# Decode attention in two parts: other half buffers for the sliding-block part, and the last keys loaded ahead of the last three value chunks

## Chip, cores, metric

One core of one Trainium2 chip. The metric is the device time of one execution in microseconds (us); the profiled span is 1.7 to 2 us shorter than the time of the same run. All runs quoted were in the fast state; the granted clock (the share of PE's full clock that the chip let it have, mean of a run) was 0.93 to 0.94.

The names in the profile: PE is the matrix engine, which does products and transposes; DVE and ACT copy and do the other arithmetic; SP issues the loads, and 16 transfer engines carry each of them. In brackets after an instruction stands the idle time before it and what ended it; "issue" means that the engine waited for nothing that the profile shows.

## The reference, cut to what matters

```python
# part A: 4 batches, 32 query heads on 8 key/value heads, the last 2048 of 8192 positions
k = jnp.repeat(k_cache[:, :, Sk - W:, :], rep, axis=1)
v = jnp.repeat(v_cache[:, :, Sk - W:, :], rep, axis=1)
scores = jnp.einsum("bhqd,bhkd->bhqk", q, k) * (Dh ** -0.5)
p = _softmax(scores, axis=-1)
o = jnp.einsum("bhqk,bhkd->bhqd", p, v)        # then @ wo
# part B: the same with 32 key/value heads and all 8192 positions
return jnp.concatenate([a, b], axis=-1)
```

One query position a batch, so every key and value is read once: 570 MB in bf16, and 587 MB with the weights. The time is that of a stream, if the stream never stops: 1366 us at the 430 GB/s of before's full slices.

## The kernel before: the parts that matter

The work is cut into 72 chunks: 0 to 7 are part A (2 MB of keys, 2 MB of values each), 8 to 71 are part B (4 MB and 4 MB). One tensor `kv` of ten half buffers (2 MB each) holds all loads in flight. An A load takes one half, from a list; a B load takes two, keys in 0-1 or 2-3, values in 4-5 or 6-7, by turns. Halves 8 and 9 serve only A and the first query weights.

```python
HALF_A = {"k": (3, 8, 0, 1, 2), "v": (7, 9, 4, 5, 6)}

def take(load, at, n, release):          # a load waits for what last read its halves
    waits = []
    for i in range(at, at + n):
        waits += held[i]
        held[i] = [release]
    half_of[load] = at
    return waits

def dma_kv(kind, c):
    ...
    at = HALF_A[kind][c % 5] if ch["ab"] == 0 else (0 if kind == "k" else 4) + 2 * (c % 2)
    waits = take((kind, c), at, 1 if ch["ab"] == 0 else 2,
                 ("T", ch["s_last"]) if kind == "k" else ("pv", c))
    ...      # the values of chunk 71 come in four pieces: LASTV = (64, 32, 16, 16) of 128 tiles

loads = [("k", c + 1) for c in range(NC - 1)]
for c in range(NC):
    loads.insert(2 * c + 1, ("v", c))     # k1 v0 k2 v1 ... k71 v70 v71
```

SP issues all these loads in this order. Keys are released by `("T", ...)`, the last transpose of the chunk on PE; values by `("pv", c)`, the last product with them. For each chunk PE does `keys_part(c)` (128 transposes in B, 64 in A, 8 to a group, each group copied out by DVE or ACT, and the scores two groups behind), then `values_part(c - 1, c)` (the products of the chunk before, with the last scores and the softmax statistics of this one in between):

```python
for c in range(NC):
    keys_part(c)
    ...
    values_part(c - 1 if c else None, c)
emit_wos(NC - 1)
norm_sum(NC - 1)
for g in range(chunks[NC - 1]["NG"]):
    emit_pv(NC - 1, g)
pv_done(NC - 1)
emit_fin(NC - 1)
```

PE's program is a loop over the periods of two chunks that are alike (`sch.mark()` at every even B chunk); what comes before chunk 12 and from chunk 70 on stands as straight code.

Of the kernel before, what the change touches and what calls it, by code (L numbers as in the profile page):

```python
# [116 lines left out]
def bass_concat_heads__sliding_block_cached__mha_block_cached__decode_kernel(  # L117
# [23 lines left out]
    chunks = []  # L141
# [6 lines left out]
    NC = len(chunks)  # L148
    NCA = Hkv
# [21 lines left out]
    with ExitStack() as es:  # L171
# [65 lines left out]

        half_of = {}
        held = [[] for _ in range(NH)]
        HALF_A = {"k": (3, 8, 0, 1, 2), "v": (7, 9, 4, 5, 6)}  # L240

        def take(load, at, n, release):
            waits = []
# [53 lines left out]

        loads = [("k", c + 1) for c in range(NC - 1)]
        for c in range(NC):
            loads.insert(2 * c + 1, ("v", c))  # L300
        wo_next = 0
        for kind, c in loads:
            dma_kv(kind, c)
# [22 lines left out]
        def emit_xT():  # L326
            for ab in (0, 1):
                xv = xs[:, ab, :].rearrange("b (p r) -> b r p", r=KC)
                for r in range(KC):
                    o = xtps[:, (ab * KC + r) * NB:(ab * KC + r + 1) * NB]  # L330
                    pe_mm(o, xv[:, r, :], identb[0:NB, 0:NB], transpose=True,
                          waits=[("x", 0), ("x", 1), "c_identb"], key="xTmm" if (ab == 1 and r == KC - 1) else None)
            sch.add("dve", lambda e: e.tensor_copy(xT[:, :, :], xtps.rearrange("p (a x) -> p a x", a=2)),
                    waits=["xTmm"], key="xT")
            ms_read[:] = ["xT"]
# [59 lines left out]
        def emit_S(s):  # L395
            c, g = groups[s]
            ch = chunks[c]
            for t in range(TG):
                j = g * TG + t
                if ch["ab"] == 1:  # L400
                    bank, o0 = c % 2, 2 * j
                else:
                    bank, o0 = j // HT, 16 * (j % HT)

                n = min(NW, 512 - o0)
                q = qb[:, c % 2, 0:n] if ch["ab"] == 1 else qs[:, 16 * ch["g"]:16 * ch["g"] + n]
                waits = []
                if t == 0:
                    waits = [("ev", s)] + sc_read[bank]
                    if g == 0:  # L410
                        waits += [("qb", c) if ch["ab"] == 1 else ("q", 0)]
                    sc_read[bank] = []
                pe_mm(sc[:, bank, o0:o0 + n], kt[:, s % NKT, t * P:(t + 1) * P], q,
                      waits=waits, key=("S", s) if t == TG - 1 else None)
# [22 lines left out]
        def stats_rowmax(c):  # L437
            ch = chunks[c]
            m, C = c % NSM, ch["C"]
            if ch["ab"] == 0:  # L440
                src = sA[:, c % 2, :].rearrange("p (j c) -> p c j", c=C)
                sch.add("dve", lambda e: e.tensor_reduce(out=rm[:, m, 0:C], in_=src, axis=AX.X, op=ALU.max),  # L442
                        waits=[("so", c, 0), ("so", c, 1)], key=("rowmax", c))
                return
            for u, pp in HALVES:
                src = sc[pp, c % 2, 0:NTB * 2].rearrange("p (j u) -> p u j", u=2)[:, u, :]
                sch.add("dve", lambda e, src=src, pp=pp: e.tensor_reduce(out=rm[pp, m, 0:1], in_=src, axis=AX.X, op=ALU.max),  # L447
                        waits=[("S", ch["s_last"])], key=("rowmax", c) if u == 1 else None)
# [58 lines left out]
        def emit_pv(c, g):  # L507
            ch = chunks[c]
            UC = ch["UC"]
            base = 16 * (c % NSM) if ch["ab"] == 0 else 2 * ((c - NCA) % 2)  # L510
            for t in range(TG):
                j = g * TG + t
                n = NW if c < NC - 1 else UC
                waits = [("exp", c)] + po_read if j == 0 else []
                if c == NC - 1:
                    waits += [("vl", j)] if ("vl", j) in sch.tk else []
                elif j == 0:
                    waits += [("v", c)]
                pe_mm(po[:, base:base + n], tile_of("v", c, j), pbt[ch["ab"]][:, c % NPB, j * UC:j * UC + n],
                      start=j == 0, stop=j == ch["NT"] - 1, waits=waits, key=("pv", c) if j == ch["NT"] - 1 else None)  # L520
# [31 lines left out]
        def emit_fin(c):  # L552
            ch = chunks[c]
            ab = ch["ab"]
            p0 = 0 if ab == 1 else 32
            if ab == 1:
                ov = oz[:, :].rearrange("p (b u) -> p b u", u=2)
                ops = [(ov[:, :, u], wos[:, u, :]) for u in range(2)]
                waits = [("oT", c), ("wos", c)]
            else:  # L560
                w = wor[:, ch["wo"] % NWO, :].rearrange("p (hl n) -> p hl n", hl=4)
                ov = oT[:, c % NSM, :].rearrange("p (u c) -> p u c", c=REP)
                ops = [(ov[:, :, cc], w[:, cc, :]) for cc in range(REP)]
                waits = [("oT", c), ("wo", ch["wo"])]
            lastc = NC - 1 if ab == 1 else NCA - 1
            firstc = NCA + 1 if ab == 1 else 0
            for i, (l, r) in enumerate(ops):
                pe_mm(fin[p0:p0 + NB, :], l, r, start=i == 0 and c == firstc, stop=i == len(ops) - 1 and c == lastc,
                      waits=waits if i == 0 else [], key=("fin", c) if i == len(ops) - 1 else None)
            if c == lastc:  # L570
                sch.add("dve", lambda e: e.tensor_copy(outsb[p0:p0 + NB, :], fin[p0:p0 + NB, :]), waits=[("fin", c)], key=("osb", ab))
                sch.add_dma("sp" if ab == 1 else "act",
                            lambda e: e.dma_start(out[:, 0, ab * DO:(ab + 1) * DO], outsb[p0:p0 + NB, :]),
                            "d_o%d" % ab, waits=[("osb", ab)], key=("out", ab))


        def pv_done(c):
            if c < NCA or (c - NCA) % 2:
                norm_out(c)

        def keys_part(c):
            ch = chunks[c]
            if c >= NCA and (c - NCA) % 2 == 0:
                sch.mark()
            for g in range(ch["NG"]):
                emit_T(ch["s"] + g)
                if g >= SLAG:
                    emit_S(ch["s"] + g - SLAG)
                if ch["ab"] == 0 and g == HT // TG - 1 + SLAG:
                    scores_out(c, 0)  # L590

                if 1 <= c <= NCA and g == 2:
                    stats_gmax(c - 1)
                if 1 <= c <= NCA and g == 3:
                    stats_exp(c - 1)
                if 1 <= c <= NCA and g == 6:
                    norm_sum(c - 1)
                if 2 <= c <= NCA + 1 and g == 4:
                    emit_fin(c - 2)
                if c > NCA + 1 and (c - NCA) % 2 == 0 and g == 4:  # L600
                    emit_wos(c - 1)
                if c > NCA + 1 and (c - NCA) % 2 == 0 and g == 6:
                    norm_sum(c - 1)
                if c > NCA + 2 and (c - NCA) % 2 == 1 and g == 4:
                    emit_fin(c - 2)

        def values_part(c, nxt):

            ch = chunks[nxt]
            late = list(range(ch["s_last"] + 1 - SLAG, ch["s_last"] + 1))  # L610
            todo = {2: lambda: emit_S(late[0]), 5: lambda: scores_last(nxt)}
            if ch["ab"] == 1:
                todo[10] = lambda: stats_gmax(nxt)
                todo[14] = lambda: stats_exp(nxt)
            if nxt + 1 < NC and nxt + 1 >= NCA:
                todo[7] = lambda: emit_qb(nxt + 1)

            def scores_last(c):
                emit_S(late[1])
                if chunks[c]["ab"] == 0:  # L620
                    scores_out(c, 1)
                stats_rowmax(c)

            for g in range(16):
                if c is not None and g < chunks[c]["NG"]:
                    emit_pv(c, g)
                    if g == chunks[c]["NG"] - 1:
                        pv_done(c)
                if g in todo:
                    todo[g]()  # L630

        emit_xT()
        emit_q(0)
        for c in range(NC):
            keys_part(c)
            if c == 0:
                emit_q(1)
            values_part(c - 1 if c else None, c)
        emit_wos(NC - 1)
        norm_sum(NC - 1)  # L640
        for g in range(chunks[NC - 1]["NG"]):
            emit_pv(NC - 1, g)
        pv_done(NC - 1)
        emit_fin(NC - 1)

        @block.sync
# [54 lines left out]
```

## Time and profile before

| | before |
|---|---|
| time, median of 4 runs beside the change | 1403.47 us (1402.05 to 1403.87) |
| profiled span (of another run, 1404.69 us) | 1402.8 us |
| busy: PE, DVE, ACT | 84%, 48%, 30% |
| HBM read, mean rate over the span | 587.21 MB, 419 GB/s |
| keys 8 landed / values 8 landed | 130.5 / 162.3 us |
| values 70 landed / last piece of values 71 landed | 1385.6 / 1395.4 us |
| last product with values 71 done | 1399.0 us |

"Landed" is the last of the 16 increments that a load leaves in the trace, one for each transfer engine (in before 16 packets of SP's loads were in flight for 88% of the time); the engines are not level, and the slowest sets it (values 70 in before: first increment at 1376.7 us, last at 1385.6). The profile's lines are in the prediction below. PE's speed changes too: in before its granted clock was 0.50 from 1376 to 1380 us, where the first 24 transposes of chunk 71 took 2.74 us, and 1.00 from 1356.5 to 1358, where 24 of chunk 70 took 1.51. Read the row of GB/s first: where it stands at 430 (425 to 435 in slices 6 to 39) the stream sets the time, the transfer engines' busy share being 1.00 to 1.01 from 160 to 1380 us, and a gain must come from the slices where it does not.

### The profile page before, as it was taken

The numbers are of one execution on the slowest core, as the hardware profiler recorded it, in microseconds if no ns is written. First come the engines' busy times: TensorE is split into PE (matmuls) and PEld (weight loads), VectorE is DVE, ScalarE is ACT, GpSimd is POOL, SyncE is SP. The second block draws the span as 40 slices with busy tenths as digits, with TensorE's granted clock in tenths as the row PEclk, the third lists the DMA queues.
The fourth block names the chain that finished last, engine by engine and source line by source line (L and its number), as shares of the span: only waits on it lengthen the run. The fifth ranks groups of instructions, "written<-read, shape, count | busy, mean of one in ns | idle before, by whom it ended". The sixth has DMA issues, their size and how long they took to land.

```text
span 1402.8 us, 57072 instructions
## 1 busy us (share of the span) xinstructions
PE 1175.2 (84%) x26768; PEld 1133.0 (81%) x26768; DVE 673.4 (48%) x1327; ACT 423.3 (30%) x617; POOL 19.2 (1%) x22
## 2 busy tenths in 40 slices
PE   4876796989888898888888888888988798888887
PEld 4765786888888898888888888888988788888887
DVE  2775453544444454444544444444544354444553
ACT  1332232333323233223332233323333233223331
POOL 1111000000000000000000000000000000000000
PEclk9998998999999999999999999999999999999998
DMA  9997899999999999999999999999999999999995
GB/s 400 416 413 286 357 429 428 432 432 425 431 430 433 430 433 430 431 428 434 432 431 430 428 432 433 434 427 430 432 431 433 429 430 433 433 426 435 431 431 251
DMA packets 29992, 588.02 MB, mean 419 GB/s; under 512 B 2656, under 2 KB 10864, under 8 KB 11120
## 3 DMA queue, kind: packets, MB, share of 16 engines
q1 hardware_dynamic: 29912, 587.22, 98.0%
q8 instruction: 40, 0.66, 0.2%
q14 instruction: 16, 0.13, 0.0%
q10 hardware_dynamic: 24, 0.01, 0.0%
HBM read 587.21 MB, written 0.01 MB: 419 GB/s over the span
## 4 chain that ended last, share of the span: by engine, by line
DMA 62%; PE 33%; DVE 4%; issue 1%; ACT 0%; SPq 0%; ACTq 0%; DVEq 0%
DMA kv<-in_B_k_cache_dram 59%; PE tr L320 20%; PE sc L322 9%; PE po L322 2%; DMA kv<-in_A_k_cache_dram 1%; PE fin L322 1%; DMA kv<-in_A_wq_dram 1%; DVE kt L383 1%; DVE rsa L500 1%; DVE sA L432 1%; PE ms L322 1%; DVE sel L425 1%; DVE rm L442 0%; DVE sA L489 0%; DVE rs L498 0%
## 5 line engine op out<-in xcount | busy, mean ns | idle before, releaser
L320 PE MATMUL tr<-identb,kv 128*128 128x128 bf16 x8704 | 705.1, 232 | 176.6 <-DMA kv<-in_B_k_cache_dram 168.5
L383 DVE COPY kt<-tr 128x1024 bf16<-128x1024 bf16 x736 | 502.8, 691 | 491.8 <-PE tr L320 487.5
L320 PEld LDWEIGHTS tr<-identb,kv 128*128 128x128 bf16 x8704 | 560.2, 105 | 203.2 <-issue 110.9
L381 ACT ACTIVATE kt<-tr 128x1024 bf16<-128x1024 bf16 x352 | 360.5, 1024 | 668.7 <-PE tr L320 666.1
L322 PE MATMUL sc<-qb,kt 128*128 128x64 bf16 x8192 | 424.7, 197 | 0.9 <-DVE kt L383 0.7
L322 PEld LDWEIGHTS sc<-qb,kt 128*128 128x128 bf16 x8192 | 351.4, 101 | 2.8 <-DVE kt L383 0.9
L322 PE MATMUL po<-pbb,kv 128*128 128x64 bf16 (+1 forms) x8192 | 290.1, 191 | 12.5 <-issue 12.3
L322 PEld LDWEIGHTS po<-pbb,kv 128*128 128x128 bf16 x8192 | 263.0, 97 | 13.2 <-issue 11.1
L481 ACT ACTIVATE pbb<-sc,negb 64x128 bf16<-64x128 f32 x128 | 51.2, 400 | 297.8 <-DVE negb L471 297.0
L447 DVE TENSOR_REDUCE rm<-sc 64x1 f32<-64x128 f32 x128 | 37.0, 289 | 94.1 <-PE sc L322 93.2
L322 PE MATMUL sc<-qs,kt 128*128 128x64 bf16 (+3 forms) x512 | 26.3, 197 | 16.5 <-DVE kt L383 16.5
L471 DVE COPY negb<-ms 128x1 f32<-128x1 f32 (+1 forms) x72 | 11.4, 159 | 56.6 <-PE ms L322 56.6
L322 PEld LDWEIGHTS sc<-qs,kt 128*128 128x128 bf16 x512 | 21.2, 101 | 19.6 <-DVE kt L383 19.4
L459 DVE TENSOR_REDUCE gm<-ms 1x2 f32<-1x128 f32 (+1 forms) x72 | 20.1, 278 | 31.9 <-PE ms L320 31.7
L322 PE MATMUL ms<-identf,gx 1*128 1x1 f32 (+1 forms) x144 | 27.6, 259 | 0.8 <-DVE gx L463 0.8
L322 PEld LDWEIGHTS ms<-identf,gx 1*128 1x128 f32 (+1 forms) x144 | 21.5, 186 | 5.1 <-DVE gx L463 1.1
L481 ACT ACTIVATION_READ_ACCUMULATOR pbb<-sc,negb 64x1 f32 x128 | 23.7, 185 | 0.0
L322 PE MATMUL po<-pba,kv 128*128 128x64 bf16 x512 | 20.0, 197 | 0.0
L322 PE MATMUL fin<-wos,oz 128*4 128x512 bf16 x64 | 19.6, 388 | 0.3 <-DVE oz L541 0.3
L320 PE MATMUL ms<-identf,rm 128*1 128x128 f32 (+1 forms) x72 | 19.6, 273 | 0.2 <-DVE rm L447 0.2
L322 PEld LDWEIGHTS po<-pba,kv 128*128 128x128 bf16 x512 | 17.6, 101 | 0.0
L432 DVE TENSOR_REDUCE sA<-sel 128x128 f32<-128x512 f32 x16 | 17.0, 1061 | 0.5
(46 smaller groups left out, 179.4 us busy)
## 6 DMA issues: line engine op xcount, KB each, us to landing
kv<-in_B_k_cache_dram SPq DMA_DIRECT2D x64, 4096.0 KB, 27.5
kv<-in_B_v_cache_dram SPq DMA_DIRECT2D x63, 4096.0 KB, 32.1
kv<-in_A_k_cache_dram SPq DMA_DIRECT2D x8, 2048.0 KB, 25.8
kv<-in_A_v_cache_dram SPq DMA_DIRECT2D x8, 2048.0 KB, 25.5
kv<-in_A_wq_dram SPq DMA_DIRECT2D x1, 4096.0 KB, 12.3
kv<-in_B_wq_dram SPq DMA_DIRECT2D x1, 4096.0 KB, 27.2
wor<-in_A_wo_dram SPq DMA_DIRECT2D x8, 512.0 KB, 21.3
wor<-in_B_wo_dram SPq DMA_DIRECT2D x8, 512.0 KB, 33.3
```

The costliest lines, as they stand in the source:

```text
L320: emit = lambda e: e.transpose(o, l, r)
L322: emit = lambda e: e.matmul(o, l, r, start=start, stop=stop)
L381: sch.add("act", lambda e: e.activation(dst, src, ACTF.Copy), waits=waits, key=("ev", s))
L383: sch.add("dve", lambda e: e.tensor_copy(dst, src), waits=waits, key=("ev", s))
L425: sch.add("dve", lambda e: e.tensor_tensor(out=sel[:, :].rearrange("p (j b c) -> p j b c", b=NB, c=REP), in0=sc[:, half, :].rearrange("p ( ...
L432: sch.add("dve", lambda e: e.tensor_reduce(out=dst, in_=sel[:, :].rearrange("p (j b c) -> p j c b", b=NB, c=REP), axis=AX.X, op=ALU.add), ...
L447: sch.add("dve", lambda e, src=src, pp=pp: e.tensor_reduce(out=rm[pp, m, 0:1], in_=src, axis=AX.X, op=ALU.max), waits=[("S", ch["s_last"]) ...
L459: sch.add("dve", lambda e: e.tensor_reduce(out=gm[0:C, m, 0:U], in_=src, axis=AX.X, op=ALU.max), waits=[("trm", c)], key=("gmax", c))
L471: sch.add("dve", lambda e: e.tensor_copy(negb[:, m, 0:C], ms[:, col:col + C]), waits=[("bc", c)], key=("negb", c))
L481: sch.add("act", lambda e, src=src, pp=pp, n=n, u=u: e.activation(pbv[pp, :, u], src, ACTF.Exp, bias=negb[pp, m, 0:1], scale=scale, accum_ ...
L500: sch.add("dve", lambda e: e.tensor_tensor(out=rst[0][:, m, :].rearrange("p (b c) -> p b c", b=NB), in0=bcast(rs4[:, m, :], [[0, NB], [1, ...
```

## The change

It intends two things: the first B loads find halves whose A data was used up early, and at the end the keys of chunk 71 come ahead of the last three value chunks, so that only products remain behind the last load.

```diff
-        HALF_A = {"k": (3, 8, 0, 1, 2), "v": (7, 9, 4, 5, 6)}
+        HALF_A = {"k": (2, 3, 8, 0, 1), "v": (6, 7, 9, 4, 5)}
...
-            loads.insert(2 * c + 1, ("v", c))
+            loads.insert(2 * c + 1 if c < NC - 3 else len(loads), ("v", c))
...  (in keys_part: what values_part(c - 1) would have held for the chunk before the last)
-                if c > NCA + 2 and (c - NCA) % 2 == 1 and g == 4:
+                if NC - 1 > c > NCA + 2 and (c - NCA) % 2 == 1 and g == 4:
                     emit_fin(c - 2)
+                if c == NC - 1 and g in (0, 1):
+                    emit_S(chunks[c - 1]["s_last"] - 1 + g)
+                if c == NC - 1 and g == 1:
+                    stats_rowmax(c - 1)
+                if c == NC - 1 and g == 5:
+                    stats_gmax(c - 1)
+                if c == NC - 1 and g == 9:
+                    stats_exp(c - 1)
...
+        def values_only(c0, c1):
+            for c in range(c0, c1):
+                for g in range(chunks[c]["NG"]):
+                    emit_pv(c, g)
+                pv_done(c)
...
-            values_part(c - 1 if c else None, c)
+            if c == NC - 2:
+                emit_qb(c + 1)
+            else:
+                values_part(None if c == 0 else c - 1 if c < NC - 1 else c - 2, c)
+            if c == NC - 1:
+                values_only(c - 1, c)
+        emit_fin(NC - 3)
         emit_wos(NC - 1)
         norm_sum(NC - 1)
-        for g in range(chunks[NC - 1]["NG"]):
-            emit_pv(NC - 1, g)
-        pv_done(NC - 1)
+        values_only(NC - 1, NC)
         emit_fin(NC - 1)
```

## The prediction

> **What bounds the kernel now.** I read the page first, for the share of each engine over time. Slice by slice, 35.07 us each:
>
> ```profile
> DMA  9997899999999999999999999999999999999995
> GB/s 400 416 413 286 357 429 428 432 432 425 431 430 433 430 433 430 431 428 434 432 431 430 428 432 433 434 427 430 432 431 433 429 430 433 433 426 435 431 431 251
> HBM read 587.21 MB, written 0.01 MB: 419 GB/s over the span
> ```
>
> The 16 transfer engines are full from the sixth slice to the last but one, at 430 GB/s. PE is 84% busy and DVE 48%, and on the page's chain 62% is waiting for loads. So the kernel streams 587 MB, and a change can win only where the stream is not full: slices 4 and 5 (286 and 357) and the last (251). At 430 the whole takes 587.2 / 0.430 = 1366 us, so all holes and ends together are 1402.8 - 1366 = 37 us, or 2.6%. Part of that cannot go (A's shorter rows at about 415, the start, the last arithmetic).
>
> Next the table of stretches around the first hole (after the window come its length, five engines' busy time with instruction counts, granted clock, DMA share, GB/s):
>
> ```profile
> 100.00:105.00 5.00, 4.20 (x69) 3.26 (x69) 4.19 (x7) 2.08 (x3) 1.89 (x1) 1.00 0.99 417
> ...
> 108.00:111.00 3.00, 1.63 (x34) 1.46 (x32) 2.93 (x6) 1.02 (x1) 0.00 (x0) 1.00 0.06 23
> 111.00:119.00 8.00, 6.89 (x140) 5.71 (x136) 6.39 (x12) 3.49 (x4) 1.89 (x1) 1.00 0.22 59
> ...
> 146.00:149.00 3.00, 2.78 (x90) 2.56 (x86) 1.48 (x5) 0.41 (x1) 0.00 (x0) 1.00 0.00 0
> ```
>
> There are two holes, about 107 to 119 and 145 to 150. Then the issuing engine's timeline (start, length, instruction):
>
> ```profile
> 89.82 0.37 SPq L268 DMA_DIRECT2D wor<-in_A_wo_dram  x1
> 117.18 0.35 SPq L290 DMA_DIRECT2D kv<-in_B_k_cache_dram  x1
> ...
> 118.80 0.63 SPq L290 DMA_DIRECT2D kv<-in_B_k_cache_dram  x1
> 148.63 0.34 SPq L290 DMA_DIRECT2D kv<-in_B_v_cache_dram  x1
> ```
>
> SP issues in order. After 89.82 it stands at the first B keys (chunk 8) for 27 us, then at the first B values for 30 us. The cause is in the program: keys 8 go to halves 0 and 1, and half 0 holds the last A keys (chunk 7: the list 3,8,0,1,2 gives it index 7 mod 5 = 2). Its transposes end at 117.2, where the load starts. Values 8 go to halves 4 and 5, and half 4 holds values 7, read only after the transposes of chunk 8, ending 148.6.
>
> Last the end, on PE's timeline:
>
> ```profile
> 1375.89 2.74 PE L320 MATMUL tr<-identb,kv 128*128 128x128 bf16 x24 [1.55 <-DMA kv<-in_B_k_cache_dram]
> ...
> 1395.42 0.39 PE L322 MATMUL ms<-rsb,onesf 128*128 128x4 f32 x2 [0.86 <-ACT pbb L481]
> 1395.66 3.36 PE L322 MATMUL po<-pbb,kv 128*128 128x2 bf16 x128
> 1399.35 1.02 PE L322 MATMUL fin<-wos,oz 128*4 128x512 bf16 x2 [0.33 <-DVE oz L541]
> ```
>
> The last keys land at 1375.9; transposes, scores and values 70 occupy PE until 1395.4; all 128 value products of chunk 71 follow. The trace's landing records (16 increments a load, one for each transfer engine) put the last value piece at 1395.4, the same moment. Arithmetic and stream end level, so removing arithmetic alone saves less than the tail looks like.
>
> [...] late in the kernel a load's first engine is done 8.8 us and its median one 5.6 us before its last. [...] At 1375.89 24 transposes take 2.74 us, against 1.51 at 1356.44; the idle before it was 1.55 us and the one before 1356.44 was 1.88 us[...].
>
> **Part 1, the new lists of halves.** No instruction is added; only addresses and waits change. Keys 8 now wait for the transposes of chunks 3 and 4, keys 9 for 5 and 6, values 8 for products 3 and 4, values 9 for 5 and 6. The early halves 8/9 and 4/5, first used by the query weights, are reused a load later, so nothing early waits longer.
>
> New issue times, on before's clock: keys 8 directly after the output weights at 89.82; values 7 behind them; output weights 7 wait for fin 4 (PE timeline: 100.9); keys 9 for the transposes of chunk 6 (about 107.3); values 8 at once. What stands in the queue? By 89.8 SP has issued 43.5 MB, and the stretches sum to 36.8 MB moved: 6.8 MB left. With keys 8 and values 7 (6.3 MB) it lasts 13.1 / 0.43 = 30 us, to about 120; keys 9 and values 8, there by 108, bring it to 141. PE leaves A at 119.9, keys 8 are there by then (landing below), its transposes take some 14 us, so keys 10 are issued near 134, before the queue is dry at 141. Keys 11 come near 150, against 162. From there it is the steady state. So both holes close completely.
>
> Their size, by landings: the load before the first hole lands at 109.5 and keys 8 at 130.5. A 4 MB load directly behind another lands 9.7 us later, so 21.0 - 9.7 = 11.3. Keys 9 land at 146.6 and values 8 at 162.3: 15.7 - 9.7 = 6.0. Sum **17.3 us**. Check by bytes: 18.07 MB move in 100 to 160, which need 42.0 us at 430: 18.0 lost. I take off about 0.6, because the drain also lets the slowest transfer engine catch up (spread 3.5 us before, 1.7 after), a lag that a full queue keeps. **16.7 us**, all of it on the path, as the stream is full from 160 on.
>
> **Part 2, the last keys first.** The order keys 70, values 69, keys 71, values 70, values 71 becomes keys 70, 71, values 69, 70, 71. PE now does transposes 70, transposes 71, then values 69, 70, 71. Bytes and products are unchanged. The gain is that value products of chunk 71 can follow the four pieces as they land, instead of all standing behind the softmax: after the last landing only 16 products remain (16 x 25 ns = 0.4 us, about 0.8 at half clock), then the unchanged 3.8 us from the last product (1399.0) to the end (1402.8).
>
> The cost: values 71 use the halves of values 69, whose products now come after transposes 71. On before's clock: keys 70 land 1356.4, transposes to 1367.2 (10.7 us), transposes 71 with their share of statistics 11.3 us to 1378.4, values 69 with the last scores 5.1 us to 1383.5. Only then are values 71 issued, 9 us later than before (1374.4). Values 70 end on the slowest engine at 1385.6, so its queue just does not run dry, but the other engines' do. From an empty queue 4 MB took 11.6 (first engine) to 13.7 us (last) in the first holes. That gives a last landing between 1395.3 and 1397.2. In before PE lost 2.1 us to "issue" at 1370; if this falls before values 69, up to 1399. I choose 1396.8: end 1396.8 + 0.8 + 3.8 = 1401.4, a gain of **1.4 us** (range 3 gained to 1 lost).
>
> Sum 16.7 + 1.4 = 18.1; 1403.6 - 18.1 = **1385.5 us**, 1.3% faster.
>
> **The rivals.** (a) The wait only moves: PE, bound in A by its copies at 12.15 us a chunk (output weights are issued at 65.52, 77.67 and 89.82, each freed by a chunk's end), starts B late and frees halves too late; a hole of some 5 us reopens near 140. For: PE's late end of A. Against: 7 us of margin above. Time 1390. (b) The tail turns worse, as values 71 are issued into an empty queue and their landing, not the softmax, ends the kernel: 1388. For: the 9 us later issue; against: the slowest engine is still busy. (c) The lag of the slowest engine is re-set by the holes and worth more than I took: 1387 to 1388. (d) The other way, late hits fall on a different engine and spread evens out: 1382.
>
> **Range and chances.** The first part is arithmetic on a full queue, uncertain by 2 us; the tail by 2 us; rivals a and b are one in ten each. Range 1382 to 1389.5. Over 2% would need 28 us, more than both holes (18) and the tail's 3 together: 0.02. Slower by 2% has no mechanism: 0.01.
>
> **What would show it.** Right: slices 4 and 5 at 410 or more GB/s; the first B keys issued near 90 and landing near 119; PE's 10.4 us wait at 120 gone; the stretch 100 to 160 with DMA share 0.97 or more; the four last pieces issued 3 to 5 us before PE's last wait, and PE waiting for them. Wrong: any stretch below 0.9 between 105 and 300 (step 1's queue count failed); last landing over 20 us from the issue of the last pieces or end more than 6 us after it (step 2); a stream rate other than 430 in the middle.

## The result

**1389.03 us** (median of 4 runs, 1388.57 to 1390.24) against 1403.47; ratio 0.990, interval 0.9883 to 0.9917. A ratio here is the mean time of one kernel's fast runs over the mean of the other's of the same rounds, so not quite the ratio of the medians. 14.4 us were won; 18.1 had been forecast.

The page of the changed kernel, busy share of the transfer engines and their rate in 40 slices:

```profile
DMA  9999999999999999999999999999999999999995
GB/s 398 417 415 424 426 429 423 432 425 436 430 432 433 428 433 428 434 427 432 430 436 429 429 429 435 432 429 430 430 432 430 430 430 435 427 428 431 434 417 237
```

Slices 4 and 5 went from 286 and 357 to 424 and 426. The end did not improve: the last two slices are now 417 and 237 (431 and 251 before). The stretches of the two holes (columns as in the prediction):

```profile
108.00:111.00 3.00, 1.63 (x33) 1.45 (x30) 2.95 (x6) 1.02 (x1) 0.00 (x0) 1.00 1.17 487
111.00:119.00 8.00, 6.91 (x147) 5.73 (x145) 5.92 (x11) 3.49 (x4) 1.89 (x1) 1.00 0.94 401
...
146.00:149.00 3.00, 3.00 (x72) 2.93 (x70) 1.92 (x3) 1.66 (x2) 0.00 (x0) 1.00 1.04 432
```

From 23, 59 and 0 GB/s to 487, 401 and 432: both holes are gone. SP's timeline says why, and also shows what became of the end:

```profile
89.77 1.42 SPq L290 DMA_DIRECT2D kv<-in_B_k_cache_dram  x1
...
104.58 1.46 SPq L290 DMA_DIRECT2D kv<-in_B_k_cache_dram  x1
106.09 0.43 SPq L290 DMA_DIRECT2D kv<-in_B_v_cache_dram  x1
...
1370.51 1.85 SPq L287 DMA_DIRECT2D kv<-in_B_v_cache_dram  x4
```

Keys 8 are issued at 89.8 instead of 117.2, values 8 at 106.1 instead of 148.6. The four pieces of values 71, though, leave at 1370.5. Values 70 had landed at 1368.1, so the stream had run dry. PE's timeline of the end:

```profile
1339.05 2.74 PE L320 MATMUL tr<-identb,kv 128*128 128x128 bf16 x24 [3.39 <-DMA kv<-in_B_k_cache_dram]
...
1351.85 0.61 PE L320 MATMUL tr<-identb,kv 128*128 128x128 bf16 x8 [0.64 <-DVE qb L392]
...
1358.51 0.29 PE L322 MATMUL sc<-qb,kt 128*128 128x64 bf16 x4 [1.75 <-issue]
...
1379.12 1.84 PE L322 MATMUL po<-pbb,kv 128*128 128x2 bf16 x64 [3.62 <-DMA kv<-in_B_v_cache_dram]
...
1384.11 0.58 PE L322 MATMUL po<-pbb,kv 128*128 128x2 bf16 x16 [0.62 <-DMA kv<-in_B_v_cache_dram]
1385.02 1.01 PE L322 MATMUL fin<-wos,oz 128*4 128x512 bf16 x2 [0.33 <-DVE oz L541]
```

Where softmax work stood before, PE now waits for values: 3.62 us for the first piece, 0.62 for the last. Along the landings:

| us | before | changed | earlier by |
|---|---|---|---|
| keys 8 landed | 130.5 | 119.7 | 10.8 |
| values 8 landed | 162.3 | 146.9 | 15.4 |
| values 70 landed | 1385.6 | 1368.1 | 17.5 |
| last piece of values 71 landed | 1395.4 | 1384.1 | 11.3 |
| last product done | 1399.0 | 1384.7 | 14.3 |
| span | 1402.8 | 1388.5 | 14.3 |

So the stream was 17.5 us ahead until the last load, which then gave back 6.2; of these 3.0 came back since only 16 products follow the last landing. The first part seemed worth more than the whole change, and the second part to cost 3 us. That was my theory for the experiments; the rival was that the second part is neutral and the first worth 14.

### The profile page after: what moved, and what is told of

Same layout as the page of the kernel before. It is cut to its first block, busy times and chain, and to the rows that moved or that the text cites. A ratio compares the mean times of both kernels' runs of the same rounds, so it can differ in the third digit from the quotient of the medians.

```text
span 1388.5 us, 57015 instructions
## 1 busy us (share of the span) xinstructions
PE 1167.4 (84%) x26768; PEld 1124.6 (81%) x26768; DVE 673.0 (48%) x1327; ACT 422.9 (30%) x617; POOL 19.2 (1%) x22
## 4 chain that ended last, share of the span: by engine, by line
DMA 60%; PE 33%; DVE 5%; issue 2%; ACT 0%; SPq 0%; DVEq 0%
DMA kv<-in_B_k_cache_dram 57%; PE tr L320 21%; PE sc L322 9%; DMA kv<-in_A_k_cache_dram 2%; PE po L322 2%; DVE kt L383 1%; DVE sA L432 1%; DMA kv<-in_B_v_cache_dram 1%; DVE rsa L500 1%; PE ms L322 1%; DVE sel L425 1%; DVE rm L442 0%; DVE sA L489 0%; DVE rs L498 0%; ACT eA L492 0%
## 5 line engine op out<-in xcount | busy, mean ns | idle before, releaser
L322 PEld LDWEIGHTS po<-pbb,kv 128*128 128x128 bf16 x8192 | 263.8, 97 | 15.8 <-issue 8.2
L463 DVE TENSOR_SCALAR gx<-gm 1x128 f32<-1x128 f32 (+1 forms) x72 | 16.0, 222 | 2.5
```

Source lines behind the costliest of these rows:

```text
L322: emit = lambda e: e.matmul(o, l, r, start=start, stop=stop)
L463: sch.add("dve", lambda e: e.tensor_scalar(out=dst, in0=gv, scalar1=-scale, scalar2=None, op0=ALU.mult), waits=[("gmax", c)], key=("gx", c))
```

## The experiments

All are timed against the kernel before, in the same rounds. All results were correct.

### The lists alone

```diff
-        HALF_A = {"k": (3, 8, 0, 1, 2), "v": (7, 9, 4, 5, 6)}
+        HALF_A = {"k": (2, 3, 8, 0, 1), "v": (6, 7, 9, 4, 5)}
```

> Only the new lists of halves; load order and the end as before. My theory from the two traces: the two holes near 107 and 145 us are worth 17.4 us (values 70 land at 1385.6 before and 1368.1 after), and the new end of the kernel costs about 3 us. Then this one takes 1403.5 - 17.4 = 1386 us and beats the whole change by 3 us. Rival: the holes were worth only the 14.4 us that the whole change gained and the end is neutral: 1389 us, level with the whole change.

Measured: 1388.35 us (1387.96 to 1388.50), ratio 0.9887, against 1404.08. Between the two theories: at 1404.08 the ratio means 15.9 us, and its interval (0.9873 to 0.9901, or 13.9 to 17.8 us) excludes neither. Values 70 landed at 1368.5 and the last piece at 1378.2, 17 us ahead of before, as expected; but the last product ended only at 1382.4. PE's timeline of this kernel:

```profile
1356.83 0.99 PE L322 MATMUL po<-pbb,kv 128*128 128x64 bf16 x28 [1.94 <-issue]
...
1375.96 0.27 PE L320 MATMUL ms<-identf,rm 128*1 128x128 f32 x1 [1.79 <-issue]
1378.68 0.39 PE L322 MATMUL ms<-rsb,onesf 128*128 128x4 f32 x2 [0.86 <-ACT pbb L481]
```

The second "issue" wait, 1.79 us, stands in the softmax of chunk 71, right on the path.

### The end alone

The whole change with the old lists.

```diff
-        HALF_A = {"k": (2, 3, 8, 0, 1), "v": (6, 7, 9, 4, 5)}
+        HALF_A = {"k": (3, 8, 0, 1, 2), "v": (7, 9, 4, 5, 6)}
```

> Only the new order of the last loads and of the last PE work; the lists of halves as before. My theory: values 71 are issued 2 us or more after values 70 have landed, and the stream stands some 6 us, of which 3 come back because only 16 products follow the last landing: 1403.5 + 3 = 1406.7 us, with about 16 us between the landing of values 70 and the last landing (9.8 before). Rival (end neutral): 1403.5 us. My own prediction of before the result (end gains 1.4): 1402 us.

Measured: 1407.37 us (1404.04 to 1409.53, 6 runs), ratio 1.0020, interval 1.0006 to 1.0035: 2.8 us slower than before. PE's timeline shows the same new wait as the whole change:

```profile
1395.82 1.86 PE L322 MATMUL po<-pbb,kv 128*128 128x2 bf16 x64 [3.72 <-DMA kv<-in_B_v_cache_dram]
```

Values 70 landed at 1386.4, values 71 were issued at 1387.1 and the last piece landed at 1400.8, 14.4 us after values 70 (expected 16; before 9.8). The interval means a loss of 0.8 to 4.9 us: the sign of my theory is shown and its size agrees; my prediction's gain (1402) is wrong.

### The whole change, values 71 in halves that are free

```diff
             at = HALF_A[kind][c % 5] if ch["ab"] == 0 else ...
+            if kind == "v" and c == NC - 1:
+                at = 8
```

> The whole change, and the values of chunk 71 go to halves 8 and 9, which nothing has used since the A part, so that their load waits for nothing late. My theory: it is issued directly behind values 70 near 1336, lands 9.8 us after them at about 1378, and the end follows 4.4 us later: a span of 1382.4, a time of about 1383 us, 6 us under the whole change. Rival (the loss at the end comes from the reordering of PE or from the four small pieces, not from the wait for the halves): 1388 to 1389 us.

Measured: 1389.80 us (1387.92 to 1390.38), ratio 0.9898. The step about the stream held, the time did not follow. SP's timeline:

```profile
1338.20 1.98 SPq L289 DMA_DIRECT2D kv<-in_B_v_cache_dram  x4
```

32 us earlier than in the whole change, and the last piece landed at 1378.5, 9.8 us after values 70. But the profiled span was 1386.2, not 1382.4. That was moreover the fastest of the four runs; by the medians nothing was won against the whole change (ratio 0.9898 here, 0.9900 there), and the rival's number was the nearer. PE's timeline:

```profile
1358.15 0.29 PE L324 MATMUL sc<-qb,kt 128*128 128x64 bf16 x4 [1.75 <-issue]
...
1371.10 1.08 PE L324 MATMUL po<-pbb,kv 128*128 128x64 bf16 x31 [1.98 <-issue]
...
1373.29 5.03 PE L324 MATMUL po<-pbb,kv 128*128 128x64 bf16 x128 [0.26 <-DVE oz L543]
...
1379.02 3.35 PE L324 MATMUL po<-pbb,kv 128*128 128x2 bf16 x128
```

PE reaches the products of chunk 71 at 1379.0, when all pieces are there, and does all 128 at one go. Its own way there had grown: the "issue" waits, and 5.03 us for the products of values 70 (3.92 in the whole change; the granted clock was 0.76 from 1374 on). My theory of a single cause at the end fell. There are two limits of nearly the same length: the late load of values 71 and, right behind it, PE.

### The lists, the old end, values 71 in the free halves

```diff
(against the lists alone)
             at = HALF_A[kind][c % 5] if ch["ab"] == 0 else ...
+            if kind == "v" and c == NC - 1:
+                at = 8
```

> The new lists of halves, the old order of loads and of PE work, and the values of chunk 71 in halves 8 and 9. In before the softmax of chunk 71 on PE and the last landing came at the same moment, so an earlier issue alone should give nothing: 1386 us, within 1 us of the run with the lists alone, the 128 products of chunk 71 still in one piece behind the softmax. If instead the end is set by the landing alone, it ends with the run of the whole change with spare halves, at 1383 us.

Measured: 1388.50 us (1388.18 to 1389.06), ratio 0.9889: level with the lists alone, as expected (both some 2 us above the 1386 that I had named). With the old end an earlier issue of values 71 is worth nothing. It did not land earlier either (last piece at 1379.5, against 1378.2 with the lists alone), so what an earlier landing would be worth here was not tested.

### One list at a time

```diff
+ keys alone:    HALF_A = {"k": (2, 3, 8, 0, 1), "v": (7, 9, 4, 5, 6)}
+ values alone:  HALF_A = {"k": (3, 8, 0, 1, 2), "v": (6, 7, 9, 4, 5)}
```

> Before with the new list for the keys alone. Keys 8 are issued near 90 and land at 119.7; values 8 still wait for the products of values 7, which follow the transposes of chunk 8, near 138.5; the queue holds keys 9 until 135.8, so a hole of about 6 us stays there: values 8 land near 152 (147.1 with both lists). Gain 10 to 11 us: 1393 to 1394 us. Rival (the holes are one wait, and closing the first closes the second): 1388.4 us as with both lists.

> Before with the new list for the values alone. Keys 8 are still issued when the transposes of chunk 7 end (117.2) and land at 130.5; values 8 are issued at once and land 9.7 us behind keys 9. Gain 6 us: 1398 us. Rival (the second hole follows from the first and cannot be closed alone): 1404 us.

Measured, against 1404.19: keys alone 1393.47 us (1392.09 to 1394.96), ratio 0.9928, 10.1 us won; values alone 1399.47 us (1398.15 to 1399.99), ratio 0.9967, 4.6 us won. SP's timeline with the keys' list alone, then with the values' list alone:

```profile
90.28 0.51 SPq L290 DMA_DIRECT2D kv<-in_B_k_cache_dram  x1
...
137.54 0.34 SPq L290 DMA_DIRECT2D kv<-in_B_v_cache_dram  x1
```

```profile
116.92 0.35 SPq L290 DMA_DIRECT2D kv<-in_B_k_cache_dram  x1
...
119.22 0.44 SPq L290 DMA_DIRECT2D kv<-in_B_v_cache_dram  x1
```

Each list moves its own issue and leaves the other one late. Values 8 landed at 151.1 and 156.4 (162.3 before): 11.2 and 5.9 us, the two sizes that the prediction read from the landings. The holes are two waits, not one. Together the lists brought 15.2 at that place, not 17.1: where the queue did not run dry the slowest engine kept its lag (in the changed kernel the first engine was 3.9 us ahead of the last at 110.0 us, 3.9 at keys 8 and 5.2 at values 8; at values 8 it was 2.1 in before and 1.9 with either list alone).

### The lists, with PE's loop over the last period

```diff
-            if nxt + 1 < NC and nxt + 1 >= NCA:
+            if nxt + 1 >= NCA:                      # one DVE copy that nothing reads
                 todo[7] = lambda: emit_qb(nxt + 1)
...
             values_part(c - 1 if c else None, c)
+        sch.mark()                                  # chunks 70 and 71 join the loop
```

(`emit_qb` takes the columns of chunk 71 again in that case.)

> The lists alone, and PE's loop runs over the last period too (one more mark, and one DVE copy that nothing reads makes the period regular)[...]. Theory: the idle that the profile names issue (1.94 us before the last part of values 69 and 1.79 us within values 70 in the run with the lists alone)[...] the packets of the instruction queue stop at 294 us in before and start again at 1364. Then both waits go, the 128 products of chunk 71 start near 1377 instead of 1378.9, and the time is 1386 to 1386.7 us, 2 us under the lists alone. Rival (these waits are PE's own and come wherever the code stands): 1388.4 us.

Measured: 1386.24 us (1384.90 to 1387.72), ratio 0.9875, as expected and 2 us under the lists alone. The instruction queue after 1340 us (packets, MB, share), with the lists alone and then with the longer loop:

```profile
q8 instruction: 7, 0.11, 1.0%
```

```profile
q8 instruction: 1, 0.02, 0.1%
```

All waits of PE after 1330 us in the kernel with the longer loop (total, times, longest):

```profile
PE tr L320 <- DMA kv<-in_B_k_cache_dram: 4.4, 2, 2.2
PE ms L322 <- ACT pbb L482: 0.9, 1, 0.9
PE fin L322 <- DVE oz L542: 0.3, 1, 0.3
```

No "issue" is left; the products of chunk 71 start at 1377.3 (1378.9 with the lists alone) and end at 1380.7, 1.1 us after the last landing at 1379.6. So the waits that the profile calls "issue" went here with straight code and its seven packets (1.94 and 1.79 us, against none with one packet). What makes PE wait there was not shown; what the waits cost is taken up again below.

### The whole change again, and the two others beside it

> The whole change, unaltered, for comparison on the same chip: 1389 us by its first result. Against the run with the lists alone (1388.35) my corrected theory says that the end of the change costs about 1 us, not 3: with the spare halves the stream's loss at the end was gone (last landing 1378.5 against 1384.1) and the kernel still ended at 1386.2, as PE was then late.

Measured: 1390.33 us (1389.26 to 1391.91), ratio 0.9907. The same kernel, the lists alone and the longer loop then ran on one chip, with no further edit:

> The whole change once more, beside the next two on one chip: 1389 to 1390.5 us.

> The lists alone once more, beside the whole change on one chip. If the second part costs at the end what the traces show (span 1386.2 against 1387.4 and 1388.5), this is 1 to 2 us faster than the whole change: 1388 to 1388.5 us. Rival (the second part is neutral): the same within 0.5 us.

> The lists with the longer PE loop once more, on the same chip as the two before: 1386 us, 2 us under the lists alone and 3 to 4 under the whole change. Rival (its first result was a lucky chip): level with the lists alone.

| on one chip, before 1404.26 us | median (range) us | ratio, interval |
|---|---|---|
| whole change | 1390.93 (1388.26 to 1393.66) | 0.9909 (0.9896 to 0.9923) |
| lists alone | 1389.12 (1388.27 to 1390.82) | 0.9896 (0.9881 to 0.9911) |
| lists, longer loop | 1386.37 (1384.57 to 1387.99) | 0.9870 (0.9855 to 0.9885) |

The lists alone are 1.8 us under the whole change; the intervals overlap, but the order is the same in the other comparison (1388.35 and 1390.33, on two chips), and the end alone was clearly slower than before. The longer loop is 4.6 us under the whole change, and these intervals do not overlap: it is the best version with a result confirmed on two chips. Part of the spread within one kernel may be PE's speed at the end, an estimate from two traces. PE's timeline at the transposes of chunk 71, first in the 1386.4 us run of the longer loop, then in its 1388.0 us run:

```profile
1360.15 1.51 PE L320 MATMUL tr<-identb,kv 128*128 128x128 bf16 x24 [2.19 <-DMA kv<-in_B_k_cache_dram]
```

```profile
1360.27 2.10 PE L320 MATMUL tr<-identb,kv 128*128 128x128 bf16 x24 [2.39 <-DMA kv<-in_B_k_cache_dram]
```

Nearly the same wait (2.19 and 2.39 us), but the second time PE came out of it slower (2.10 us for 24 transposes against 1.51), and its products of chunk 71 started 1.66 us later. The lists alone on the same chip:

```profile
1357.39 0.99 PE L322 MATMUL po<-pbb,kv 128*128 128x64 bf16 x28 [2.45 <-issue]
...
1360.21 2.74 PE L320 MATMUL tr<-identb,kv 128*128 128x128 bf16 x24 [1.18 <-DMA kv<-in_B_k_cache_dram]
```

The only "issue" wait at this end was over before keys 71 landed, so it was not itself on the path; what is seen behind it is a slow start, 2.74 us for 24 transposes against 1.51. From the first transpose of chunk 71 to its first product with values it was 20.2 us in the first trace of the lists alone (1.79 us of "issue" in it), 19.8 in this one (none in it), and 17.1 and 18.7 with the longer loop. That the longer loop is faster is shown; that the "issue" waits alone make the 2 us is not, and whether they also bring on the slow starts was not tested.

### The spare halves, with one DVE copy moved

The whole change with values 71 in halves 8 and 9, and `emit_qb(71)` ahead of `keys_part(70)` instead of behind it.

```diff
+            if c == NC - 2:
+                emit_qb(c + 1)
             keys_part(c)
...
-            if c == NC - 2:
-                emit_qb(c + 1)
-            else:
+            if c != NC - 2:
                 values_part(...)
```

> The whole change with the values of chunk 71 in the spare halves, and the small DVE copy of the query columns for chunk 71 put ahead of the transposes of chunk 70, so that PE no longer waits 0.64 us for the queue behind it. Theory: with the spare halves the end is PE's, so the time falls by that 0.6 us and no more: 1389.2 us against 1389.8, the last landing unchanged near 1378.5. Rival (the landing still ends the kernel): no change.

Measured: 1387.20 us (1384.63 to 1388.05), ratio 0.9875. Neither expectation: the wait that I wanted to remove is still there under another name,

```profile
1350.72 0.61 PE L322 MATMUL tr<-identb,kv 128*128 128x128 bf16 x8 [0.64 <-DVE kt L385]
```

so the copy never was its cause, and the profiled span (1385.8) is only 0.4 us under the one without the move. Why the other runs are faster by 2.6 us than those of the spare halves without it, on another chip, stays open. On its own chip this kernel is 3.7 us under the whole change (intervals 0.9860 to 0.9890 and 0.9896 to 0.9923) and level with the longer loop. So the spare halves won nothing in one comparison and 3.7 us in the other; what the late issue of values 71 costs in time stays open between the two.

## Why the prediction was right or wrong

The time fell in the range (1389.03 in 1382 to 1389.5), near its upper end; the middle was 3.5 us too low. The class (within 2%) and the reasons for the first part held. The second part had the wrong sign: a gain of 1.4 us was said, and the end alone lost 2.8. That the time still fell in the range is owed to the upper end, which left room for rival (b), and not to that step.

1. **What bounds the kernel: right.** The gain came from the two holes alone, and the stream in between kept its 427 to 431 GB/s. Whether a higher rate could be had was not tested.
2. **The queue count: right.** Keys 8 were issued at 89.8, keys 9 at 104.6 (said 107), keys 10 at 134.4 (said 134), keys 11 at 150.5 (said 150); no stretch between 105 and 155 fell under a share of 0.94. Rival (a) did not happen.
3. **The size of the holes: right.** 11.3 and 6.0 were said; one list alone gave 11.2 and 5.9 at the landing of values 8. For both 16.7 was said on the path; the lists alone gave 15.9 and 14.6 us (ratios 0.9887 and 0.9896). The deduction for the slowest engine was too small at that place: 0.6 was taken and 1.3 to 2.1 seen (17.1 less the 15.0 to 15.8 at values 8, over the traces with both lists). At the landing of values 70 the same traces were 15.6 to 17.5 us ahead, so the 16.7 lies among them; all of this is measured from one trace of before.
4. **The end, "a gain of 1.4 us": wrong, and the step that failed is the issue time of values 71.** "On before's clock" it was 1383.5, which is 1366.0 in the changed kernel (17.5 earlier). It was 1370.5. The terms: transposes 70, 10.7 said, 12.8 measured (a start at half the clock, 0.50 granted from 1339 to 1341 us and 2.74 us for the first 24 transposes against 1.51, and a 0.64 us wait); transposes 71, 11.3 said, 13.7 measured (1.75 and 0.23 us of "issue" in them); values 69, 5.1 said, 4.9 measured. So "its queue just does not run dry" was false by 2.4 us, and from the empty queue the load took 13.6 us, at the top of the 11.6 to 13.7 that I had read. A start at a clock of 0.50 (2.74 us at 1375.9) and an "issue" wait (2.10 us, before 1372.7) both stood in before's trace; I left them out of the middle estimate although the plan had only 2.1 us of slack (1385.6 less 1383.5). (The lower end of its range for the last landing, 1395.3, is a slip: 1383.5 + 11.6 is 1395.1.) None of the signs of a wrong second step that the prediction named came true: the last piece landed 13.6 us after the first was issued, not over 20, and the end followed 4.4 us later, not over 6. None of them asked when the load would be issued.
5. **The last 4.6 us: right**, 4.4 measured between last landing and end.
6. **Rival (b), the worse end: it is what happened.** It said 1388 and was given one chance in ten; the argument against it, "the slowest engine is still busy", is the failed step of point 4. How much of the loss is the late issue is not settled. With the spare halves the last piece landed 5.6 us earlier than in the whole change, but the time was the same in one comparison and 3.7 us shorter in the other. In both of their traces PE reached the products of chunk 71 only when all pieces were there (1379.0 and 1378.7, landed 1378.5 and 1378.1), so PE was almost as late as the load.
7. **Rival (c) was partly right**: at values 8 the lag of the slowest engine was under-counted by about 1 us. It does not explain the miss of the whole change, which was 17.5 us ahead at values 70. What makes one engine lag was not tested.

## What to carry to other kernels

In a kernel that streams, follow the issuing queue in order: here one load, keys 8, stood at SP for 27 us and held back all behind it, and handing out the same buffers in another order closed the hole at no cost. Before moving work to the end of a kernel, write down when the last load can be issued, with the waits that the trace shows put in; the plan here ended nearly level with the queue (2.1 us of slack), and the load left 2.4 us after the queue had run dry. And keep the last period inside the loop if it can be made regular: here the end as straight code took seven instruction packets, the longer loop one, and the longer loop was 2.1 and 2.8 us faster.

## What the traces showed besides

- Seven packets of the instruction queue q8 after 1340 us (0.11 MB in all) came with "issue" waits on PE, of 1.94 and 1.79 us in one trace of the lists alone (the transfer engines' busy share was 1.01 from 1350 to 1358 us, around the first, and 0.15 from 1374 to 1380, around the second); the other trace of the lists alone had one such wait, of 2.45 us. With the last period in the loop one packet and no such wait was left, and the time fell by 2.1 us (on two chips) and 2.8 us (on one), not all of it shown to be these waits.
- PE's loop of two chunks (over 1500 instructions) ran from 300 to 1340 us without a packet of q8, both with the lists alone and with the longer loop; q14, the other instruction queue, had 12 packets (0.10 MB) in that time.
- The 16 engines of a load finished apart: in the changed kernel by 3.9 us at 110 us and by 9.4 us at 1339, and by 1.7 to 2.1 us for a load issued into an empty queue (keys 8 and values 8 in before, the pieces of values 71 in the changed kernel). In before the distance was 3.5 us ahead of the first hole and 1.7 behind it; in the changed kernel, without the hole, it was 3.9 at both places.
- From issue to landing, 4 MB that SP issued into an empty queue took 13.3 us (keys 8 in before), 13.7 (values 8 in before) and 13.6 (the four pieces of values 71 in the changed kernel), against 9.7 us for each further load behind another.
